# Blocked attention and two MLPs on one core: the first attention pass ordered per engine by a planner in the kernel, block sums of v on VectorE

## The chip, the cores and the metric

The kernel runs on one core of one Trainium2 chip. The metric is device time in microseconds (us), the median of the runs. Five engines run side by side, each through a queue of its own that it never reorders: TensorE (PE; its weight loads are listed as PEld), VectorE (DVE), ScalarE (ACT), GpSimd (POOL) and SyncE (SP), which here only issues transfers. An engine that waits for another holds up everything behind the waiting instruction.

## The reference

```python
k_sum = k.reshape(B, H, nb, block, D).max(axis=3)       # block = 32
v_sum = v.reshape(B, H, nb, block, D).mean(axis=3)
scores_l = scale * q @ k.T          # kept where |pos_q - pos_k| < 16
scores_s = scale * q @ k_sum.T + np.log(block)
a = softmax(concat([masked scores_l, scores_s]))        # 1e-9 added to the sum
x = a @ concat([v, v_sum])                              # (B*S, H*D) = (1536, 512)
h = x @ w_in                        # 512 -> 2048
x = (max(h, 0) + alpha * min(h, 0)) @ w_out             # first MLP
h = x @ w2_in
out = (h * sigmoid(h)) @ w2_out                         # second MLP
```

q, k and v are (2, 8, 768, 64), all float32. Each query sees a window of its neighbours and the 24 block sums of its head.

## The kernel before

**Tiling.** The 1536 tokens are six blocks of 256 (three per batch), the eight heads four pairs. One *item* is a block and a pair: 24 items, of which the first eight are blocks 0 and 1 pair by pair, then blocks 2 to 5. An item runs through all engines: `scores` (PE, tile `sc`, eight matmuls of 64 queries by 120 keys, the 120 being 24 block maxima and 96 neighbours), scaling and mask (DVE, `t`), row maximum (DVE, `nm`), `exps` (ACT, `e`, sums into `sm`), 1e-9 added to the sums and reciprocal (DVE, `sm` and `rs`), `normalize` (POOL, `e`), `turn` (PE, `pt`; copied by ACT to `pT`), `values` (PE, `o`), and the split of the result in two float32r halves (ACT `xh`, DVE `xl`). Once per batch and pair come `prep_k` (DVE, L465, block maxima of k, copied six times at L471), `prep_v1` (POOL halves the 32 elements of a block twice at L482, DVE sums the last eight at L485, `vr`) and `prep_v2` (PE transpose `pv`, four ACT copies into `vs`).

**The MLPs.** Every float32 product is made of three float32r matmuls of halves (`three`, L281 to L283). A weight piece is loaded as 64-bit numbers and converted by three DVE instructions (L142, L146, L149), an ACT cast (`wh`) and, in the first pass, a POOL subtraction (`wl`, L156). The first of the four column chunks of the first MLP is done block by block beside attention ("dense" work below): 48 matmuls of 128x256 for the inputs of a block, activation (ACT `g` and `m`, DVE L328, ACT `gh`, POOL `gl` at L337), and 48 for its outputs. Everything later is matmuls of 128x512, four chunks for each MLP; the second MLP takes some of its products by a seven-product scheme.

**What sets the order of the first pass.** Each operation is entered in a list with a key (item number plus a constant such as `AT_TURN`); the list is walked in the order of the keys, and the framework then places each instruction on its engine by a timeline of its own. So the three conversion instructions, for example, come apart in VectorE's queue. Only block 0's inputs are accumulated pair by pair as items finish (`first_in`); blocks 1 to 5 wait until all four pairs are there.

```python
AT_KEYS, AT_SUMS, AT_MEANS, AT_SPREAD = -1.1, 1.3, 2.2, 3.2
AT_EXPS, AT_NORM, AT_TURN, AT_VALUES = 0.1, 0.3, 1.8, 3.2
for _, _, f, a in sorted(ops, key=lambda o: o[:2]):
    f(*a)
```

Of the kernel before, what the change touches and what calls it, by code (L numbers as in the profile page):

```python
# [25 lines left out]
AT_KEYS, AT_SUMS, AT_MEANS, AT_SPREAD = -1.1, 1.3, 2.2, 3.2  # L26
AT_EXPS, AT_NORM, AT_TURN, AT_VALUES = 0.1, 0.3, 1.8, 3.2
AT_IN = 5.3
AT_LATER, ITEM_STEP = 3.5, 0.8
CONV, CONV_STEP = -1.4, 0.6  # L30
CONV2, CONV2_STEP = 14.0, 1.5
BATCH, BATCH_STEP = 5.8, 2.0
NQ = 6
STAGE = 2


@with_exitstack
def tile_blocks_attention_mlps(
# [19 lines left out]
    KEYS = P + 2 * PAD  # L58
# [61 lines left out]
    def conv_next(eng):  # L120
# [33 lines left out]
        def rest():  # L154
            nc.scalar.copy(out=hi, in_=w)  # L155
            eng.tensor_tensor(out=lo, in0=w, in1=hi, op=ALU.subtract)  # L156
# [5 lines left out]
        return rest  # L162
# [115 lines left out]
    def three(ps, a, b, first, last):  # L278

        (ah, all_), (bh, bl) = a, b  # L280
        nc.tensor.matmul(ps, all_, bh, start=first, stop=False)  # L281
        nc.tensor.matmul(ps, ah, bl, start=False, stop=False)  # L282
        nc.tensor.matmul(ps, ah, bh, start=False, stop=last)  # L283
# [3 lines left out]
    def in_k(u, i, k, ps):  # L287
        l, ch, t0, n, _ = u
        c = slice(i * P, (i + 1) * P)
        hi, lo = pieces[l, ch, 0, k]  # L290
        three(
            ps, (hi[:, c], lo[:, c]), (xh[:, k, t0:t0 + n], xl[:, k, t0:t0 + n]),
            k == 0, k == KT - 1,
        )
# [9 lines left out]
    def activate(u, i, ni, banks):  # L304

# [14 lines left out]
        if l == 0:  # L320
            m = gp.tile([P, 512], F32, tag="m", name="m", bufs=1 if early else 2)
            w = ni * n // len(banks)
# [3 lines left out]
            for j in range(ni):  # L326
# [5 lines left out]
        else:  # L332
            nc.scalar.activation(out=g, in_=banks[0], func=AF.Silu)

        def rest():
            nc.scalar.copy(out=gh, in_=g)  # L336
            (nc.gpsimd if early else nc.vector).tensor_tensor(out=gl, in0=g, in1=gh, op=ALU.subtract)  # L337

        pending.append(rest)
# [80 lines left out]
    def convert(eng):  # L420
        r = conv_next(eng)
        if r is not None:
            pending.append(r)
            load_next()

    NG = NBLK * NPAIR
    with ExitStack() as scope0:
# [7 lines left out]
        mask = cst[:, P:]  # L435

        kt_t, vt_t, vs_t, q_t = {}, {}, {}, {}

        def load_k(b, p):

            t = kv.tile([P, NTWO + 1, NB + KEYS], F32, tag="kT", name="kT")
            nc.sync.dma_start(out=t[:, :NTWO, NB:], in_=kT[b, p])
            kt_t[b, p] = t

        def load_v(b, p):
# [5 lines left out]
            vt_t[b, p] = t  # L451
            t = kv.tile([NC, NSUB, P], F32, tag="vs", name="vs")
            vs_t[b, p] = t
            nc.sync.dma_start(out=t[NB:, 0::2], in_=vw[b, p, 0])
            nc.sync.dma_start(out=t[:WIN, 1::2], in_=vw[b, p, 1])
# [7 lines left out]
        def prep_k(b, p):  # L463
            t = kt_t[b, p]
            nc.vector.tensor_reduce(  # L465
                out=t[:, 0, :NB].rearrange("p (n m) -> p n m", n=NTWO),
                in_=t[:, :NTWO, NB + PAD:NB + PAD + P].rearrange("p n (m i) -> p n m i", i=BLOCK),
# [7 lines left out]
        vr_t = {}  # L475

        def prep_v1(b, p):

            t = kv.tile([P, NB], F32, tag="vr", name="vr", bufs=2)
            v = vt_t.pop((b, p)).rearrange("p (n i) -> p n i", i=BLOCK)  # L480
# [7 lines left out]
        def prep_v2(b, p):  # L488
            s_ = vs_t[b, p]
# [3 lines left out]
            def spread(s0, s1):  # L493
                for at in (s_[:NB, 2 * s0:2 * s1:2], s_[WIN:, 2 * s0 + 1:2 * s1:2]):
                    nc.scalar.activation(
                        out=at,
                        in_=pt[:NB, 0:P].unsqueeze(1).to_broadcast([NB, s1 - s0, P]),
                        func=AF.Copy,
                        scale=1.0 / BLOCK,
                    )  # L500

            spread(0, QB // P)
            return lambda: spread(QB // P, NTWO)

        e_t, pt_t, sums, t_t = {}, {}, {}, {}

        def where(n):
            blk, p = order[n]
            b, j = divmod(blk, BPB)
            return blk, p, b, j  # L510

        def scores(n):
            blk, p, b, j = where(n)
            q_, k_ = q_t.pop((blk, p)), kt_t[b, p].rearrange("p n c -> p (n c)")

            ps = ps_s.tile([P, 2, 512], F32, tag="s", name="sc")
            for i in range(2):
                for h in range(2):
                    hp = slice(h * D, (h + 1) * D)
                    for s in range(2):  # L520

                        w0 = (2 * j + i) * (NB + KEYS) + s * (NB + SUB)
                        nc.tensor.matmul(
                            ps[s * SUB:(s + 1) * SUB, h, i * NC:(i + 1) * NC],
                            q_[hp, i * P + s * SUB:i * P + (s + 1) * SUB],
                            k_[hp, w0:w0 + NC],
                            start=True,
                            stop=True,
                        )
            t = att.tile([P, 4, NC], F32, tag="t", name="t", bufs=3)  # L530
            nc.vector.scalar_tensor_tensor(  # L531
                out=t.rearrange("p (h i) c -> p h (i c)", h=2),
                in0=ps[:, :, :2 * NC],
# [5 lines left out]
            nm = att.tile([P, 4], F32, tag="nm", name="nm")  # L539
            nc.vector.tensor_reduce(out=nm, in_=t, axis=AX.X, op=ALU.max, negate=True)  # L540
            t_t[n] = t, nm

        def exps(n):
            t, nm = t_t.pop(n)
            e = att.tile([P, 4, NC], F32, tag="e", name="e", bufs=3)
            sm = att.tile([P, 4], F32, tag="sm", name="sm")
            for u in range(4):
                nc.scalar.activation(  # L548
                    out=e[:, u, :], in_=t[:, u, :], func=AF.Exp, bias=nm[:, u:u + 1],
                    accum_out=sm[:, u:u + 1],  # L550
                )
            e_t[n] = e
            sums[n] = sm

        def normalize(n):
            sm, e = sums.pop(n), e_t[n]
            nc.vector.tensor_scalar(out=sm, in0=sm, scalar1=1e-9, scalar2=None, op0=ALU.add)  # L557
            rs = att.tile([P, 4, 1], F32, tag="rs", name="rs")
            nc.vector.reciprocal(out=rs.rearrange("p u o -> p (u o)"), in_=sm)
            nc.gpsimd.tensor_tensor(out=e, in0=e, in1=rs.to_broadcast([P, 4, NC]), op=ALU.mult)  # L560

        def turn(n):
            e = e_t.pop(n)
            ps = ps_mm.tile([P, 512], F32, tag="mm", name="pt")
            for u in range(4):
                nc.tensor.transpose(ps[:NC, u * P:(u + 1) * P], e[:, u, :], ident)
            t = att.tile([NC, 512], F32, tag="pT", name="pT")
            nc.scalar.copy(out=t, in_=ps[:NC])
            pt_t[n] = t

        def values(n):
            blk, p, b, j = where(n)
            t, s_ = pt_t.pop(n), vs_t[b, p]
            ps = ps_mm.tile([P, 512], F32, tag="mm", name="o")[:, :QB]
            for i in range(2):
                for s in range(2):
                    for h in range(2):
# [7 lines left out]
                        )  # L585
            at = slice(blk * QB, (blk + 1) * QB)
            nc.scalar.copy(out=xh[:, p, at], in_=ps)  # L587
            nc.vector.tensor_tensor(out=xl[:, p, at], in0=ps, in1=xh[:, p, at], op=ALU.subtract)


# [283 lines left out]
```

## Time and profile before

| what | value |
|---|---|
| median of three runs | 608.24 us (608.11 to 608.34) |
| span of the profiled execution | 604.6 us, first to last instruction |
| around the span (median less span) | 3.6 us |
| busy share of the span: PE, DVE, ACT, POOL | 95%, 70%, 46%, 12% |
| chain that ended last, by engine | PE 82%, DVE 9%, DMA 3%, ACT 2% |

The profile gives one execution by its span alone, so its own time is taken as the span and the 3.6 us around it. Busy is not the same as full speed: a matmul's length in the trace holds its way through the array, so successive matmuls overlap, and what one costs is the distance from its start to the next one's start.

### The profile page before, as it was taken

What the parts mean: (1) busy time and instruction counts of PE and PEld (TensorE: products, weight loads), DVE (VectorE), ACT (ScalarE), POOL (GpSimd) and SP (SyncE); (2) the same over time, 40 slices, a digit from 0 to 9 for tenths busy, and PEclk for the clock granted to TensorE, in tenths of its full rate; (3) what the DMA queues carried; (4) which work ended last, traced back from release to release, by engine and by line L of the source; (5) the groups of instructions that cost most, each with busy time, mean ns of one, the idle gap of its engine ahead of it and who ended that gap; (6) DMA issues with size and microseconds to landing.
All of it is one profiled execution on the core that took longest, in us unless ns stands there. A gap on an engine that the chain in (4) does not pass through costs nothing.

```text
span 604.6 us, 8927 instructions
## 1 busy us (share of the span) xinstructions
PE 576.8 (95%) x3428; PEld 483.5 (80%) x3428; DVE 424.0 (70%) x747; ACT 277.5 (46%) x636; POOL 72.3 (12%) x69
## 2 busy tenths in 40 slices
PE   2777999999999999999999999999999999999997
PEld 1556788999888888888888888888888888888886
DVE  3899979548995484349696879885972499965312
ACT  2768977654543341424544645543621245333200
POOL 2657654232100000000000000000000000000000
PEclk9988999999999999999999999999999999999999
DMA  9958754002351040003022002333130032200112
GB/s 263 341 193 260 231 147 140 2 2 70 140 154 56 0 140 0 1 1 112 28 69 70 1 1 79 131 117 93 32 108 0 1 111 96 73 1 0 54 69 88
DMA packets 31771, 52.54 MB, mean 87 GB/s; under 512 B 2288, under 2 KB 20976, under 8 KB 31728
## 3 DMA queue, kind: packets, MB, share of 16 engines
q1 hardware_dynamic: 31728, 51.97, 27.2%
q8 instruction: 27, 0.44, 0.3%
q14 instruction: 16, 0.13, 0.1%
HBM read 48.82 MB, written 3.15 MB: 86 GB/s over the span
## 4 chain that ended last, share of the span: by engine, by line
PE 82%; DVE 9%; DMA 3%; ACT 2%; SPq 1%; issue 1%; POOL 0%; DVEq 0%; POOLq 0%
PE ps L281 27%; PE ps L282 27%; PE ps L283 27%; DVE w L146 2%; DMA y<-in_w 1%; DVE w L149 1%; DMA vs<-in_vw 1%; DVE w L142 1%; DVE t L531 1%; DVE sm L557 1%; DVE nm L540 1%; PE o L579 1%; DVE kT L465 1%; ACT e L548 1%; DMA raw<-in_w 1%
## 5 line engine op out<-in xcount | busy, mean ns | idle before, releaser
L281 PE MATMUL ps<-xh,wl 128*128 128x512 f32 (+1 forms) x352 | 127.5, 367 | 1.2 <-ACT xh L587 1.2
L282 PE MATMUL ps<-xl,wh 128*128 128x512 f32 (+1 forms) x352 | 127.9, 364 | 0.0
L283 PE MATMUL ps<-xh,wh 128*128 128x512 f32 (+1 forms) x352 | 127.4, 363 | 0.0
L282 PE MATMUL ps<-gl,wh 128*128 128x512 f32 (+1 forms) x240 | 83.3, 348 | 0.0
L283 PE MATMUL ps<-gh,wh 128*128 128x512 f32 (+1 forms) x240 | 82.9, 346 | 0.0
L281 PE MATMUL ps<-gh,wl 128*128 128x512 f32 (+1 forms) x240 | 82.5, 350 | 0.0
L336 ACT CAST gh<-g 128x512 fp32r<-128x512 f32 x96 | 59.3, 622 | 46.2 <-PE ps L283 24.2
L281 PEld LDWEIGHTS ps<-xh,wl 128*128 128x128 f32 x352 | 66.5, 191 | 12.4 <-POOL e L560 1.4
L282 PEld LDWEIGHTS ps<-xl,wh 128*128 128x128 f32 x352 | 67.3, 191 | 10.2 <-issue 0.2
L283 PE MATMUL ps<-wh,gh 128*128 128x512 f32 (+1 forms) x196 | 75.4, 385 | 0.0
L283 PEld LDWEIGHTS ps<-xh,wh 128*128 128x128 f32 x352 | 67.3, 191 | 10.1
L282 PE MATMUL ps<-wl,gh 128*128 128x512 f32 (+1 forms) x196 | 75.4, 385 | 0.0
L281 PE MATMUL ps<-wh,gl 128*128 128x512 f32 (+1 forms) x196 | 75.2, 385 | 0.1
L337 DVE TENSOR_TENSOR gl<-g,gh 128x512 fp32r<-128x512 f32 x84 | 57.5, 687 | 20.7 <-ACT gh L336 20.3
L394 DVE TENSOR_TENSOR y<-ps,y 128x512 f32<-128x512 f32 x48 | 32.8, 689 | 45.4 <-PE ps L283 45.2
L324 ACT ACTIVATE g<-ps 128x512 f32<-128x512 f32 (+1 forms) x50 | 29.0, 579 | 70.8 <-PE ps L283 69.9
L155 ACT CAST wh<-w 128x512 fp32r<-128x512 f32 x64 | 39.3, 622 | 48.0 <-DVE w L149 43.5
L328 DVE SCALAR_TENSOR_TENSOR g<-m,nal,g 128x512 f32<-128x512 f32 (+1 forms) x60 | 41.4, 705 | 25.0 <-ACT m L325 24.9
L281 PEld LDWEIGHTS ps<-gh,wl 128*128 128x128 f32 x240 | 45.2, 189 | 6.6 <-issue 0.5
L282 PEld LDWEIGHTS ps<-gl,wh 128*128 128x128 f32 x240 | 45.4, 189 | 6.1 <-POOL gl L337 0.2
L283 PEld LDWEIGHTS ps<-gh,wh 128*128 128x128 f32 x240 | 45.3, 189 | 5.6
L146 DVE SCALAR_TENSOR_TENSOR w<-raw,w 128x512 uint32<-128x512 uint32 x61 | 44.6, 741 | 0.3
(82 smaller groups left out, 867.1 us busy)
## 6 DMA issues: line engine op xcount, KB each, us to landing
raw<-in_w SPq DMA_DIRECT2D x61, 512.0 KB, 3.8
vs<-in_vw SPq DMA_DIRECT2D x16, 288.0 KB, 5.6
kT<-in_kT SPq DMA_DIRECT2D x8, 480.0 KB, 5.2
q<-in_qT SPq DMA_DIRECT2D x24, 128.0 KB, 4.1
out<-y SPq DMA_DIRECT2D x11, 256.0 KB, 2.0
y<-in_vT SPq DMA_DIRECT2D x4, 384.0 KB, 6.5
y<-in_w SPq DMA_DIRECT2D x3, 512.0 KB, 7.7
raw<-in_vT SPq DMA_DIRECT2D x4, 384.0 KB, 4.5
```

Of the source, the lines that this page charges most:

```text
L142: nc.vector.tensor_scalar(out=w, in0=high, scalar1=3, scalar2=0x3FFFFFFF, op0=ALU.logical_shift_left, op1=ALU.bitwise_and,)
L146: nc.vector.scalar_tensor_tensor(out=w, in0=high, scalar=0xC0000000, in1=w, op0=ALU.bitwise_and, op1=ALU.bitwise_or)
L149: nc.vector.scalar_tensor_tensor(out=w, in0=low, scalar=29, in1=w, op0=ALU.logical_shift_right, op1=ALU.bitwise_or)
L155: nc.scalar.copy(out=hi, in_=w)
L281: nc.tensor.matmul(ps, all_, bh, start=first, stop=False)
L282: nc.tensor.matmul(ps, ah, bl, start=False, stop=False)
L283: nc.tensor.matmul(ps, ah, bh, start=False, stop=last)
L324: nc.scalar.activation(out=g[:, j * w:(j + 1) * w], in_=ps, func=AF.Relu)
L328: nc.vector.scalar_tensor_tensor(out=g[:, at], in0=m[:, at], scalar=nal[:, f + j:f + j + 1], in1=g[:, at], op0=ALU.mult, op1=ALU.add,)
L336: nc.scalar.copy(out=gh, in_=g)
L337: (nc.gpsimd if early else nc.vector).tensor_tensor(out=gl, in0=g, in1=gh, op=ALU.subtract)
L394: nc.vector.tensor_tensor(out=at, in0=src, in1=at, op=ALU.add)
```

## The change

The first pass is cut into steps, each of one engine, with a cost, the steps that it needs, the buffers that it takes and gives, and a key. `plan()` in the kernel orders them engine by engine, before anything is issued: at each turn it takes the step that can start first, the smaller key where several can within 0.03. Steps marked `lock` (the three conversion instructions, the DVE half of the activation, and every POOL step) are never planned beside each other. The instructions are then issued in that order with the framework's reordering off (`manual_schedule`). After the pass, the framework orders as before.

Moved and changed beside the order:

- The block sums of v are one DVE reduction over 768 elements (`sum_v`, 32 at a time); POOL's 16 halving instructions go.
- k is loaded once without the overlap (800 columns, 0.41 MB, in place of 960), the maxima stand behind it, and L471's eight copies go. The scores of an item are now 4 matmuls of 128 queries by 24 maxima and 8 of 64 queries by 96 neighbours. The neighbours' v is one transfer in place of two.
- The 1e-9 lies in a second column beside the sum, and a DVE reduction over two elements adds them, where a scalar add stood.
- v's means are spread by two ACT copies in place of four.
- Blocks 0 and 1 both accumulate their inputs pair by pair. Two inputs of the next chunk (`next_in`) are issued at the end of the pass.

```diff
-AT_KEYS, AT_SUMS, AT_MEANS, AT_SPREAD = -1.1, 1.3, 2.2, 3.2
+AT_KEYS, AT_SUMS, AT_MEANS, AT_SPREAD = -1.5, 2.21, 2.18, 3.06
-    KEYS = P + 2 * PAD
+    KEYS = S + 2 * PAD
...
-            nc.vector.tensor_copy(
-                out=t[:, 1:, :NB], in_=t[:, 0:1, :NB].to_broadcast([P, NTWO, NB])
-            )
...
-            for w in (BLOCK // 2, BLOCK // 4):
-                nc.gpsimd.tensor_tensor(
-                    out=v[:, :, :w], in0=v[:, :, :w], in1=v[:, :, w:2 * w], op=ALU.add
-                )
+        def sum_v(b, p, w):
+            t = kv.tile([P, NB], F32, tag="vr", name="vr", bufs=2)
+            v = vt_t.pop((b, p)).rearrange("p (n i) -> p n i", i=BLOCK)
             nc.vector.tensor_reduce(out=t, in_=v[:, :, :w], axis=AX.X, op=ALU.add)
...
+                for h in range(2):
+                    hp = slice(h * D, (h + 1) * D)
+                    nc.tensor.matmul(
+                        ps[:, h, i * NC:i * NC + NB],
+                        q_[hp, i * P:(i + 1) * P],
+                        k_[hp, KEYS:KEYS + NB],
+                        start=True,
+                        stop=True,
+                    )
...
-            nc.vector.tensor_scalar(out=sm, in0=sm, scalar1=1e-9, scalar2=None, op0=ALU.add)
+            nc.vector.tensor_reduce(out=r, in_=sm, axis=AX.X, op=ALU.add)
+            nc.vector.reciprocal(out=r, in_=r)
...
+                step(("vr", b, p), "DVE", 0.87, [("vt", b, p)], k + AT_SUMS, sum_v, b, p, BLOCK,
+                     take=["vr"], give=["raw"] * (b > 0))
...
+            step(("cv", n), "DVE", 1.65, [("W", n)] + [("cv", n - 1)] * (n > 0), t, bits, n,
+                 take=["w"], give=["raw"] * (n >= y_w.shape[1]), lock=True)
...
+                        at = max([free[e], *(end[x] for x in after)])
+                        for r in take:
+                            at = max(at, sorted(hold[r])[take.count(r) - 1])
+                        if lock:
+                            at = max(at, locked)
...
-        for _, _, f, a in sorted(ops, key=lambda o: o[:2]):
-            f(*a)
+        with tc.manual_schedule():
+            for _, _, f, a in plan():
+                f(*a)
```

Two places show what moves. First VectorE's queue, behind the block maxima of the fourth pair; `w` is a weight being converted, `sm`, `rs` and `eps` the softmax sums and their reciprocals, `xl` the low half of an item's result. Before:

```order
L557 TENSOR_SCALAR sm<-sm 128x4
L485 TENSOR_REDUCE vr<-y 128x24
L540 TENSOR_REDUCE nm<-t 128x4
L559 RECIPROCAL rs<-sm 128x4
L142 TENSOR_SCALAR w<-raw 128x512
L146 SCALAR_TENSOR_TENSOR w<-raw,w 128x512
L149 SCALAR_TENSOR_TENSOR w<-raw,w 128x512
L142 TENSOR_SCALAR w<-raw 128x512
L557 TENSOR_SCALAR sm<-sm 128x4
L588 TENSOR_TENSOR xl<-o,xh 128x256
L146 SCALAR_TENSOR_TENSOR w<-raw,w 128x512
```

The same place in the changed kernel:

```order
L488 TENSOR_REDUCE kT<-kT 128x24
L556 SCALAR_TENSOR_TENSOR t<-sc,cst 128x480
L507 TENSOR_REDUCE vr<-y 128x24
L583 TENSOR_REDUCE rs<-eps_94 128x4
L584 RECIPROCAL rs<-rs 128x4
L567 TENSOR_REDUCE nm<-t 128x4
L627 TENSOR_TENSOR xl<-o,xh 128x256
L556 SCALAR_TENSOR_TENSOR t<-sc,cst 128x480
L146 TENSOR_SCALAR w<-y 128x512
L150 SCALAR_TENSOR_TENSOR w<-y,w 128x512
L153 SCALAR_TENSOR_TENSOR w<-y,w 128x512
```

Before, the fourth and fifth weights stand here; now it is the second, its three instructions together, and an item's steps come first. When VectorE reaches the eighth `xl`, it has finished eight conversions and most of a ninth before, four now. Second, TensorE's queue in the middle of the first eight items (`pt` a transpose, `o` the values, `ps` dense work). Before:

```order
L282 MATMUL ps<-xl,wh 128x256
L283 MATMUL ps<-xh,wh 128x256
L566 MATMUL pt<-cst,e 120x128 x4
L523 MATMUL sc<-kT,q 64x120 x8
L579 MATMUL o<-pT,vs 64x64 x8
```

and now:

```order
L612 MATMUL o<-pT,vs 64x64 x8
L287 MATMUL ps<-xh,wl 128x256
L288 MATMUL ps<-xl,wh 128x256
L289 MATMUL ps<-xh,wh 128x256
L287 MATMUL ps<-xh,wl 128x256
L288 MATMUL ps<-xl,wh 128x256
```

Dense work now follows every one of the first eight items (12 matmuls each, 96 in all), where before only block 0's 48 stood between them, sometimes split by an item's matmuls.

## Rows read from the trace of the kernel before

**Rows 1.** The profile page: its first line and busy time by engine.

```profile
span 604.6 us, 8927 instructions
PE 576.8 (95%) x3428; PEld 483.5 (80%) x3428; DVE 424.0 (70%) x747; ACT 277.5 (46%) x636; POOL 72.3 (12%) x69
```

**Rows 2.** Windows, last stretch: length, busy us of each engine, clock, DMA share, GB/s.

```profile
150.00:601.00 451.00, 450.90 (x2022) 374.51 (x2021) 307.68 (x516) 177.51 (x309) 1.53 (x1) 1.00 0.18 61
```

**Rows 3.** Timeline of TensorE, late in the pass and at the end: start, us.

```profile
117.63 0.64 PE L523 MATMUL sc<-kT,q 64*64 64x120 f32 x16
118.20 0.69 PE L579 MATMUL o<-pT,vs 120*64 120x64 f32 x16
118.82 0.65 PE L566 MATMUL pt<-cst,e 128*120 128x128 f32 x4
119.40 0.69 PE L579 MATMUL o<-pT,vs 120*64 120x64 f32 x16
...
590.05 0.39 PE L282 MATMUL ps<-wl,gh 128*128 128x512 f32 x1
...
594.13 0.39 PE L282 MATMUL ps<-wl,gh 128*128 128x512 f32 x1
...
601.03 0.28 PE L282 MATMUL ps<-wl,gh 128*128 128x256 f32 x1
601.15 0.28 PE L283 MATMUL ps<-wh,gh 128*128 128x256 f32 x1
```

**Rows 4.** Windows, VectorE alone: length, busy us and count, clock, DMA.

```profile
0.00:73.40 73.40, 61.69 (x125) 0.95 0.86 259
```

**Rows 5.** Groups by line, VectorE, first 73.4 us: busy us, mean ns, idle before.

```profile
L465 DVE TENSOR_REDUCE kT<-kT 128x24 f32<-128x768 f32 x8 | 7.5, 943 | 6.4 <-DMA kT<-in_kT 6.4
...
L557 DVE TENSOR_SCALAR sm<-sm 128x4 f32<-128x4 f32 x15 | 6.4, 425 | 0.0
```

**Rows 6.** Timeline of VectorE, 57 to 65 us: start, us.

```profile
57.25 0.93 DVE L465 TENSOR_REDUCE kT<-kT 128x24 f32<-128x768 f32 x1
58.11 0.41 DVE L588 TENSOR_TENSOR xl<-o,xh 128x256 fp32r<-128x256 f32 x1
...
58.53 0.61 DVE L540 TENSOR_REDUCE nm<-t 128x4 f32<-128x480 f32 x1
59.07 0.76 DVE L557 TENSOR_SCALAR sm<-sm 128x4 f32<-128x4 f32 x1
...
59.89 0.64 DVE L531 SCALAR_TENSOR_TENSOR t<-sc,cst 128x480 f32<-128x480 f32 x1
60.46 0.41 DVE L142 TENSOR_SCALAR w<-raw 128x512 uint32<-128x512 uint32 x1
...
61.42 1.24 DVE L146 SCALAR_TENSOR_TENSOR w<-raw,w 128x512 uint32<-128x512 uint32 x1
...
63.77 0.34 DVE L485 TENSOR_REDUCE vr<-raw 128x24 f32<-128x192 f32 x1
64.03 0.15 DVE L557 TENSOR_SCALAR sm<-sm 128x4 f32<-128x4 f32 x1
64.10 0.68 DVE L149 SCALAR_TENSOR_TENSOR w<-raw,w 128x512 uint32<-128x512 uint32 x1
64.70 0.47 DVE L328 SCALAR_TENSOR_TENSOR g<-m,nal,g 128x256 f32<-128x256 f32 x1
```

**Rows 7.** Timeline of GpSimd, same stretch: start, us.

```profile
58.82 0.98 POOL L560 TENSOR_TENSOR e<-e,rs 128x480 f32<-128x480 f32 x1
...
61.12 0.99 POOL L560 TENSOR_TENSOR e<-e,rs 128x480 f32<-128x480 f32 x1 [0.70 <-DVE rs L559]
```

**Rows 8.** Timeline of TensorE, early: start, us, and its idle time before.

```profile
5.66 1.34 PE L523 MATMUL sc<-kT,q 64*64 64x120 f32 x16 [5.66 <-DVE kT L465]
...
54.90 1.08 PE L523 MATMUL sc<-kT,q 64*64 64x120 f32 x16
```

**Rows 9.** DMA issues: KB each, median us from issue to landing.

```profile
raw<-in_vT SPq DMA_DIRECT2D x4, 384.0 KB, 4.5
```

More of the change, by code (lines that the diff above doesn't have):

```diff
@@ L304, in activate, with activation @@
     def activate(u, i, ni, banks):
+        one, two, *rest = activation(u, i, ni, banks)
+        one()
+        two()
+        pending.extend(rest)
+    def activation(u, i, ni, banks):
         l, ch, t0, n, _ = u
@@ L331, in activate, with three_, four @@
                 )
-        else:
-            nc.scalar.activation(out=g, in_=banks[0], func=AF.Silu)
-        def rest():
+        def three_():
             nc.scalar.copy(out=gh, in_=g)
+        def four():
             (nc.gpsimd if early else nc.vector).tensor_tensor(out=gl, in0=g, in1=gh, op=ALU.subtract)
-        pending.append(rest)
+        return one, two, three_, four
     turn_g = [0]
@@ L730, in seq_item, with step, load @@
-        def seq_item():
-            need(CF if seq[0][1] is in_item else 2 * CF)
-            item()
-        def more_loads():
-            for _ in range(CF):
-                ask(None)
+        where = {g: k for k, g in enumerate(order)}
+        steps = []
+        def step(name, engine, cost, after, key, f, *a, take=(), give=(), lock=False, size=0):
+            steps.append((key, len(steps), name, engine, cost, after, f, a, take, give, lock, size))
+        def load(name, key, f, *a, size, after=(), take=()):
+            step(name, "SP", 0.6, after, key, f, *a, take=take, size=size)
@@ new lines, in tile_blocks_attention_mlps @@
+        room = {"sc": 1, "mm": 6, "t": 3, "e": 3, "pT": 2, "q": NQ, "k": 4, "v": 4, "vr": 2,
+                "raw": STAGE, "w": 2, "g": 1, "gh": 3}
+        at = 0
+        n = 0
+        for p in range(NPAIR):
+            load(("k", 0, p), -100 + at, load_k, 0, p, size=0.41, take=["k"])
+            load(("q", 0, p), -100 + at + 0.1, load_q, 0, p, size=0.13, take=["q"])
+            if p == 0:
+                load("cst", -100 + at + 0.2, lambda: nc.sync.dma_start(out=cst, in_=consts), size=0.31)
+            load(("vt", 0, p), -100 + at + 0.3, load_vt, 0, p, size=0.39)
+            load(("v", 0, p), -100 + at + 0.4, load_v, 0, p, size=0.6, take=["v"])
+            load(("q", 1, p), -100 + at + 0.5, load_q, 1, p, size=0.13, take=["q"])
+            at += 1
@@ new lines, in tile_blocks_attention_mlps @@
+        for n in range(3 * CF + STAGE):
+            t = W_FIRST + n * W_STEP if n < 2 * CF else max(W_FIRST + n * W_STEP, CONV2 + (n - 2 * CF) * CONV2_STEP - W_AHEAD)
+            load(("W", n), t, load_next, size=0.52, after=[("W", n - 1)] * (n > 0),
+                 take=["raw"] * (n >= y_w.shape[1]))
+        load("al", -80, lambda: nc.sync.dma_start(out=al, in_=alpha), size=0.01)
+        step("nal", "POOL", 0.1, ["al"], 0, lambda: nc.gpsimd.tensor_scalar(out=nal, in0=al, scalar1=-1.0, scalar2=None, op0=ALU.mult))
@@ L846, in _layout @@
         "qT": turned(q),
[L847 removed]
+        "kT": kp,
         "vT": turned(v),
```

445 lines of the change are left out of this document (250 added, 195 removed).

## Prediction

> **What bounds the kernel now.** Read the profile's first page, then the windows, then the timelines. TensorE is busy 95% of the span [rows 1], and from 150 us to 601 us without a gap (450.90 of 451.00) [rows 2]. So the time is TensorE's work plus what TensorE loses, and the losses lie at the start. To size them I price each matmul by the distance from its start to the next start, late in the run, where nothing is waited for [rows 3]: a 128x512 matmul 0.2267 us (18 of them between 590.05 and 594.13), a 128x256 one 0.12, an item's scores 0.57, its values 0.62, its transposes 0.58. The program holds 1956 of the first (443.4), 600 of the second (72.0), 24 items (24 x 1.77 = 42.5) and eight small transposes (a quarter of 0.58 each, 1.2): 559.0 us. The last matmul starts at 601.15, so TensorE is done at 601.3 and has lost 42.3 us. 3.3 us of tail follow to the end of the span, and 3.6 us more make the median of 608.24, against which the sum is made.
>
> Where is the loss made? VectorE runs the first pass. Its row lengths overlap the next row by some 0.08 us, so again start to start [rows 6]: block maxima 0.86, `xl` 0.33, `nm` 0.54, `t` 0.57, a sum of v over 192 elements 0.26, an `sm` or another small row 0.07, a conversion 0.33 + 0.60 + 0.60 = 1.53, half an activation 0.40. Up to the end of the second activation of block 0, at 73.4 us, its queue holds 8 maxima (6.9), 16 `t` (9.1), 16 `nm` (8.6), 6 sums of v (1.6), 9 conversions (13.8), 11 `xl` (3.6), 4 activation halves (1.6) and 36 small rows (2.5): 47.7 us. TensorE's queue holds 15 scores, 12 transposes, 10 values, 4 small transposes and 72 dense matmuls up to the matmuls that need this activation: 30.9 us. By order alone VectorE is 47.7 - 30.9 = 16.8 us behind there. It was busy 61.69 of the 73.4 us [rows 4], so it idled 11.7, 6.4 of it until a load of k landed [rows 5], and 61.7 - 47.7 = 14.0 went into rows that were longer than their price. 16.8 + 11.7 + 14.0 = 42.5: the whole loss of the run.
>
> **The change, term by term.**
>
> *Order.* In the new queues the farthest that VectorE lies behind TensorE is at the scores of the nineteenth item, which need the eighteenth `t`. Up to it VectorE has 8 maxima (6.9), 18 `t` (10.3), 17 `nm` (9.2), 8 sums of v, 7 conversions (10.7), 12 `xl` (4.0), 6 activation halves (2.4) and 34 small rows (2.4). A sum over 768 elements does not occur before; I price it as the maximum over the same 768 [rows 6], 0.86, so 6.9 where the short sums cost 2.1: 4.8 us more work in all, bounded below by 0.26 and above by the row's whole length, 0.93. Total 52.8. TensorE has 18 scores at 0.75 (below), 14 transposes, 14 values, 7 small transposes and 120 dense matmuls: 45.7. Lag 7.1 in place of 16.8. That is the largest term: conversions come later and dense work of block 1 earlier.
>
> *Idle.* Loads of k are 0.41 MB in place of 0.48, and no sum waits for GpSimd any more; but VectorE still has nothing before the first k. 11.7 becomes 9.5, between 7 and 11.7.
>
> *Lengthened rows.* An `sm` of 0.15 took 0.76 us beside GpSimd's `e`, which ran from 58.82 to 59.80, and a conversion's second instruction 1.24 beside the `e` at 61.12, where its sister took 0.68 [rows 6, 7]. The fifteen `sm` average 425 ns, 4.1 us too long together, while the maxima average 943 beside a free 930 [rows 5, 6]: a reduction is not lengthened. The new sum of two is a reduction, so 4.1 of the 14.0 go for good. Of the other 9.9, seven conversions in place of nine would leave 7.7; GpSimd's halving, part of the cause, is gone, and the plan keeps the rest apart, but on paper only, since no semaphore does. I take 5. Against it, rows that need each other's result now stand back to back (some 37 pairs); at the 0.07 by which neighbours otherwise overlap that is 2.5, an estimate. 14.0 becomes 7.5, between 2.5 and 12.4.
>
> The Trainium skill's SBUF page ("Who interferes with whom") says that VectorE and GpSimd take one port pair by an exclusive lock, that the loser stands still, and that a `tensor_reduce` never takes part. The rows above agree. By that rule alone, were the plan's gaps kept, this term would be 2.5 and the time 589; were they not, 10.2 and 597.
>
> *Scores.* An item's sixteen records (two for a matmul) take 0.57, so 0.036 each; the new form has 24. If a record's price is fixed, an item costs 0.86; if only columns count it costs no more than before. I take 0.75, nearer the first since the narrow ones carry twice the queries: +0.18 x 24 = 4.3 us of TensorE work, between 0 and 6.8.
>
> The skill's page TensorEngine Tiling (Array Packing), "Instruction Overhead", speaks against this part: a matmul has some 60 cycles of overhead, so 24 columns cost what 60 do. By it, as an estimate, eight records of 25 ns add 0.2 us an item, 4.8 us in all, and the time would be 595. No run here has shown a 24-column matmul yet.
>
> *Free.* GpSimd's sixteen halvings and two of four spreading copies of ScalarE leave engines that are busy 12% and 46% [rows 1]; they count only through the two terms above. The eight copies of the maxima are among the small rows. One transfer of neighbours in place of two takes eight issues off SP, which I put at nothing: SP waits for buffers, not for its own issue. After the pass nothing changes, and TensorE is full there as before [rows 2].
>
> *Sum.* Loss 7.1 + 9.5 + 7.5 = 24.1 in place of 42.3. 559.0 + 4.3 + 24.1 = 587.4, plus 3.3 and 3.6: **594.3 us**, 14 less than 608.24.
>
> **Rivals.**
>
> *A new wait in the fixed order.* VectorE's sum of v for the last pair of batch 1 waits for a load that SP issues behind the neighbours' v of that pair, and that needs the buffer which the twelfth item's values free. TensorE reaches those values after some 37 us of work, at 61 with its loss; two issues and 4.5 us of landing [rows 9] give 67 to 68. VectorE is there after 51 us of work and 17 lost, at 68. There is no room: if TensorE is late, VectorE stands with all `t` behind it. Price up to one landing, 4.5: 599. For it: nothing can now be moved around a late transfer. Against it: the sums were late before as well, without stopping the pass.
>
> *The plan's gaps are not kept.* `lock` exists only in the plan. Then lengthening stays at 14.0 - 4.1 + 2.5 = 12.4, 4.9 more: 599. For it: GpSimd runs `e` at any moment when sums are ready [rows 7]. Against it: seven conversions stand where nine did.
>
> *More than forecast.* Gaps kept and the narrow scores hidden: 594.3 - 5.0 - 4.3 = 585.
>
> *Slower: TensorE stays at its lower clock.* The first scores take 1.34 us, and those at 54.90 still 1.08 [rows 8], against 0.64 for the same row later [rows 3]: 1.2 GHz after the engine had waited, 2.4 GHz when it had worked on. The granted clock of the first 73.4 us is 0.95 in the windows [rows 4], which does not show all of this. Today the low clock is covered by VectorE's lag. With only 7 us of lag it would not be: were all 45.7 us run at half speed from the start at 5.7, TensorE would be at the nineteenth scores at 97.1, having lost 51.4 in place of 24.1: 621.6. It decides from the point where 5.7 plus the work at half speed passes the loss that gives today's time (24.1 + 13.9 = 38.0), so from 32 of the 45.7 us. Against it: twelve dense matmuls now follow every early item, which is what kept the clock up late in the pass.
>
> **How the numbers follow.** Forecast (589 to 599) 0.60; more than forecast (583 to 589) 0.14; new wait 0.10; gaps not kept 0.07 (both 599 to 603, where the forecast's terms are also a little worse); low clock 0.06; several small losses that add up to no change 0.03. Less than 0.2% (1.2 us) cannot be told from no change. Faster: 0.60 + 0.14 + 0.10 + 0.07, less 0.01 for a wait at its worst, 0.90; same 0.03; slower 0.07. The bounds of the terms reach from 594.3 - 2.5 - 5.0 - 4.3 = 582.5 to 594.3 + 2.2 + 4.9 + 2.5 = 603.9; 585 to 603 leaves out the low clock, no change and the best part of the best case, together under 0.2.
>
> **What would show it.** VectorE: sums over two at 0.15 and none near 0.7; sums over 768 at 0.93; conversions of about 1.6 from start to end; idle under 10 us by 70. TensorE: its last values near 120 us with dense work of two blocks behind it, no wait over 2 us after 50, scores of 0.7 to 0.8 in full stretches. Wrong would be: scores above 0.9, groups of 1.1 beyond 40 us (low clock), VectorE waiting for `raw` around 60 to 70, or conversions still at 2 us or more.

## The result: slower, 616.3 us where 594.3 was predicted

| | median of the runs | ratio to before, 95% interval |
|---|---|---|
| before | 608.17 us (607.67 to 608.34) | |
| the change | 616.31 us (613.69 to 619.24) | 1.0135 [1.0091, 1.0179] |
| the change, measured again | 614.72 us (608.33 to 618.32) | 1.0066 [1.0029, 1.0102] |

The second set had its own executions of before (median 609.57 us), and its ratio leaves out one execution of the change that stood in a slower state of the chip (618.32). So the change is slower by 0.7 to 1.4%, and it lies 12 to 13 us outside the prediction's range (585 to 603). The profiled execution took 618.46 us, 1.76 more than its span. Every execution on record has some 1.8 us around its span, so before's profiled one (span 604.6) would have taken about 606.4, which is 1.8 us less than the median and half of the 3.6 us that the prediction put around the span.

The profile page of the change, against [rows 1]:

```profile
span 616.7 us, 9237 instructions
PE 598.2 (97%) x3620; PEld 502.8 (82%) x3620; DVE 417.4 (68%) x743; ACT 275.1 (45%) x616; POOL 55.6 (9%) x53
```

TensorE is busy 21.4 us longer and VectorE 6.6 us shorter. Windows of the change (length, busy us of PE, PEld, DVE, ACT and POOL with their instructions, granted clock, DMA share, GB/s), against [rows 2, 4]:

```profile
0.00:73.40 73.40, 61.64 (x702) 49.80 (x702) 47.73 (x104) 43.79 (x149) 19.75 (x24) 1.00 0.76 218
...
150.00:612.00 462.00, 460.76 (x2147) 384.01 (x2146) 318.67 (x536) 185.02 (x324) 4.07 (x3) 1.00 0.18 61
```

In the first 73.4 us VectorE is busy 47.73 us where it had been busy 61.69, so it idles 25.7 us there, 11.7 before. (The granted clock, the 1.00 near the end of the first line, does not show that TensorE's rows up to 45 us ran at half speed; the rows below do.) Nor are VectorE's rows long. Its groups in the first 73.4 us (busy us, mean ns, idle before), against [rows 5, 6]:

```profile
L556 DVE SCALAR_TENSOR_TENSOR t<-sc,cst 128x480 f32<-128x480 f32 x14 | 9.2, 655 | 19.6 <-PE sc L544 19.6
...
L150 DVE SCALAR_TENSOR_TENSOR w<-raw,w 128x512 uint32<-128x512 uint32 x3 | 2.1, 693 | 0.1
...
L583 DVE TENSOR_REDUCE rs<-eps 128x4 f32<-128x8 f32 x13 | 2.0, 153 | 0.0
L507 DVE TENSOR_REDUCE vr<-raw 128x24 f32<-128x768 f32 x2 | 1.9, 944 | 0.0
```

The sum over two takes 153 ns where the `sm` took 425, a conversion's second instruction 693 where one had taken 1240 (1100 on average over the six from `raw`), the new sum of v 944. Instead `t` waited 19.6 us for TensorE's scores. They are what grew. TensorE's timeline (start, length in us), one item at the lower clock, one at the upper, and the end, against [rows 3, 8]:

```profile
18.53 0.63 PE L533 MATMUL sc<-kT,q 64*128 64x24 f32 x4
19.08 0.60 PE L544 MATMUL sc<-kT,q 64*64 64x96 f32 x8
19.61 0.62 PE L533 MATMUL sc<-kT,q 64*128 64x24 f32 x4
20.16 0.60 PE L544 MATMUL sc<-kT,q 64*64 64x96 f32 x8
20.69 1.12 PE L612 MATMUL o<-pT,vs 120*64 120x64 f32 x16
...
51.28 0.41 PE L533 MATMUL sc<-kT,q 64*128 64x24 f32 x4
51.62 0.40 PE L544 MATMUL sc<-kT,q 64*64 64x96 f32 x8
51.94 0.41 PE L533 MATMUL sc<-kT,q 64*128 64x24 f32 x4
52.27 0.40 PE L544 MATMUL sc<-kT,q 64*64 64x96 f32 x8
52.60 0.65 PE L596 MATMUL pt<-cst,e 128*120 128x128 f32 x4
...
613.34 0.28 PE L289 MATMUL ps<-wh,gh 128*128 128x256 f32 x1
```

An item's scores take 52.60 - 51.28 = 1.32 us, before 0.57; at the lower clock 2.16, before 1.08. "64\*128" is the part of the array that a matmul uses, rows by columns; inside an item TensorE now goes over from one to the other three times. Values (0.62) and transposes (0.58) cost what they did. 24 x 0.75 = 18.0 us of work were added.

For each kernel below I made the same account of TensorE up to 152 us: its work over before's 559.0 us; its waits (the brackets in its timeline); and what rows at half speed took over their price at the upper clock, start to start. The fillers of e10 are matmuls on zeros, counted with the time that they took. All in us, of the profiled execution, which is one out of each kernel's scatter (e6's is among its slower ones, e17's its fastest), so these spans do not rank the kernels as the medians do:

| kernel | scores of an item | added work | waits | half speed | sum | span |
|---|---|---|---|---|---|---|
| before | 0.57 | 0 | 25.7 | 14.9 | 40.6 | 604.6 |
| the change | 1.32 | 18.0 | 14.0 | 18.6 | 50.6 | 616.7 |
| e1, old scores | 0.57 | 0 | 25.6 | 15.2 | 40.8 | 605.5 |
| e6, 64x24 scores | 0.73 | 3.8 | 22.3 | 14.5 | 40.6 | 605.4 |
| e2, grouped | 1.05 | 11.5 | 15.1 | 15.2 | 41.8 | 607.6 |
| e4, 64x120 | 1.40 | 19.9 | 14.5 | 8.7 | 43.1 | 609.0 |
| e10, e6 and fillers | 0.73 | 3.8 + 11.2 | 13.9 | 7.9 | 36.8 | 602.2 |
| e17, e6 with less VectorE work | 0.73 | 3.8 | 19.3 | 9.3 | 32.4 | 595.7 |

The span less the sum is 563.3 to 566.1 us in all eight, where before's work and tail are 562.3: 1 to 4 us are in none of the columns, and the kernels agree to 3 us. TensorE's waits fell from 25.7 to 14.0, and the longer scores added 18.0. The waits did not fall by the new order alone: with before's scores and layouts in it (e1) they are 25.6.

### The profile page after: what moved, and what is told of

It is laid out like the page before. It is cut to its first block, busy times and chain, and to the rows that moved or that the text cites. A ratio compares the mean times of both kernels' runs of the same rounds, so it can differ in the third digit from the quotient of the medians.

```text
span 616.7 us, 9237 instructions
## 1 busy us (share of the span) xinstructions
PE 598.2 (97%) x3620; PEld 502.8 (82%) x3620; DVE 417.4 (68%) x743; ACT 275.1 (45%) x616; POOL 55.6 (9%) x53
## 4 chain that ended last, share of the span: by engine, by line
PE 90%; DVE 3%; DMA 2%; ACT 2%; issue 1%; POOL 0%; SPq 0%; POOLq 0%; ACTq 0%; DVEq 0%
PE ps L287 27%; PE ps L288 27%; PE ps L289 27%; PE sc L533 3%; PE sc L544 3%; PE o L612 2%; PE pt L596 2%; DMA q<-in_qT 1%; DVE g L347 1%; DMA raw<-in_w 1%; DVE w L150 1%; ACT g L341 1%; DVE t L556 0%; POOL gl L356 0%; ACT m L342 0%
## 5 line engine op out<-in xcount | busy, mean ns | idle before, releaser
L287 PE MATMUL ps<-xh,wl 128*128 128x512 f32 (+1 forms) x352 | 131.4, 373 | 0.0
L288 PE MATMUL ps<-xl,wh 128*128 128x512 f32 (+1 forms) x352 | 129.6, 368 | 0.0
L289 PE MATMUL ps<-xh,wh 128*128 128x512 f32 (+1 forms) x352 | 129.5, 368 | 0.0
L287 PEld LDWEIGHTS ps<-xh,wl 128*128 128x128 f32 x352 | 69.2, 197 | 10.8
L288 PEld LDWEIGHTS ps<-xl,wh 128*128 128x128 f32 x352 | 69.3, 197 | 10.1 <-DVE xl L627 0.2
L289 PEld LDWEIGHTS ps<-xh,wh 128*128 128x128 f32 x352 | 69.1, 196 | 10.0
L341 ACT ACTIVATE g<-ps 128x512 f32<-128x512 f32 x48 | 28.7, 598 | 72.5 <-PE ps L289 68.8
L347 DVE SCALAR_TENSOR_TENSOR g<-m,nal,g 128x512 f32<-128x512 f32 (+1 forms) x60 | 38.8, 663 | 28.5 <-ACT m L342 28.3
L159 ACT CAST wh<-w 128x512 fp32r<-128x512 f32 x64 | 39.3, 621 | 41.6 <-DVE w L153 37.1
L574 ACT ACTIVATE e<-t,nm 128x120 f32<-128x120 f32 x96 | 36.6, 383 | 15.8 <-DVE nm L567 15.1
```

The lines of the kernel that those rows point to most:

```text
L287: i = nc.tensor.matmul(ps, all_, bh, start=first, stop=False, skip_group_check=again)
L288: nc.tensor.matmul(ps, ah, bl, start=False, stop=False, skip_group_check=again)
L289: nc.tensor.matmul(ps, ah, bh, start=False, stop=last, skip_group_check=again)
L341: nc.scalar.activation(out=g[:, j * w:(j + 1) * w], in_=ps, func=AF.Relu)
L347: nc.vector.scalar_tensor_tensor(out=g[:, at], in0=m[:, at], scalar=nal[:, f + j:f + j + 1], in1=g[:, at], op0=ALU.mult, op1=ALU.add,)
L574: nc.scalar.activation(out=e[:, u, :], in_=t[:, u, :], func=AF.Exp, bias=nm[:, u:u + 1], accum_out=sm[:, u, 0:1],)
```

## Experiments

The edits are shown in short, not word for word. Each run was timed beside before, whose median was 609.1 to 609.7 us in these sets; the ratios are to that.

### What the scores cost: e1, e2, e4, e5, e6

**e1** puts before's scores and layouts into the new order.

```diff
-    4 matmuls q[64 x 128], maxima[64 x 24];  8 matmuls q[64 x 64], window[64 x 96]
+    8 matmuls q[64 x 64], [24 maxima | 96 neighbours][64 x 120]
```

> The change with the scores of before: eight 64x120 matmuls an item instead of four 128x24 and eight 64x96, and with them the layouts of before (stacked k with its copies of the block maxima, vw in two transfers, spread in two activations an half); the planned order, VectorE's sums of v and the eps tiles stay. Theory W, a small fp32 matmul costs by the columns of its stationary tile (64 queries .07 us, 128 queries .15 to .17): an item's scores fall from 1.31 back to 0.57 us at the upper clock and from 2.16 to 1.08 at the lower, 24 x 0.74 = 17.8 us leave TensorE's work, and the time is 597 to 602 us, faster than both kernels. Rival O, the new order or the clock costs the time and the scores only show it (operands that arrive piecemeal inside an item): an item stays over 1.0 us and the time stays at 612 or above.

605.91 us (ratio to before 0.994 [0.9912, 0.9968]); an item 0.57 again. So the scores' form, with the layouts that belong to it, is the difference between slower and faster (rival O falls), but only 9 to 10 of the 18 us come through, less than theory W's 597 to 602 asked for: TensorE's waits are back at 25.6.

**e2** issues the 128x24 matmuls of both halves first.

```diff
     for i in range(2):
         for h in range(2): matmul 128x24
+    for i in range(2):
         for h in range(2):
             for s in range(2): matmul 64x96
```

> The change with the four 128x24 matmuls of an item issued first and the eight 64x96 behind them, so that TensorE goes over between the two tile shapes once inside an item instead of three times. Theory W (stationary columns): nothing changes, an item's scores 1.31 us, time within 3 us of the change (613 to 619). Rival S, each going-over between tile shapes costs: of the 0.74 us more than before, 0.28 is four records' worth each way and the rest, about 0.46, lies in four goings-over of 0.115, so two fewer give 1.08 us an item and 24 x 0.23 = 5.5 us less, 611.

606.53 us (0.9957 [0.9931, 0.9983]). TensorE's timeline of e2:

```profile
54.00 0.63 PE L533 MATMUL sc<-kT,q 64*128 64x24 f32 x8
54.56 0.56 PE L545 MATMUL sc<-kT,q 64*64 64x96 f32 x16
55.05 0.69 PE L613 MATMUL o<-pT,vs 120*64 120x64 f32 x16
```

The same matmuls take 0.56 + 0.49 = 1.05 us where they took 1.32. Only their order changed, and with it the number of goings-over, from three inside an item to one: 0.135 us each. Theory W (the columns of the stationary tile) falls, and S stands in the price (it gave 1.08). In time 8 to 10 us follow, more than the 6.5 us of work: in the profiled executions rows at half speed took 3.4 us less as well.

**e4** widens the windows; the extra columns are written over or read by nobody.

```diff
-    ps[.., i * NC + NB:(i + 1) * NC],      k_[hp, w0:w0 + WIN]
+    ps[.., i * NC + NB:(i + 1) * NC + NB], k_[hp, w0:w0 + NC]
```

> The change with every 64x96 score matmul widened to 64x120 moving columns (the 24 more land where the next 128x24 writes over them or in columns that nobody reads). Theory W (stationary columns): an item's scores stay at 1.31 us (the 64x96 records at 41 ns, as before's 64x120 had 36), time within 3 us of the change. Rival M, moving columns set the price: the sixteen records' 0.65 us grow by a quarter, 0.16 us an item, 24 x 0.16 = 3.9 us more, about 620.

612.16 us (1.006 [1.0032, 1.0088]), an item 1.40. A quarter more moving columns costs 0.08 us an item, half of rival M's price and more than W's nothing: columns count, but little. The time did not rise with it (0.6% above before, the change 0.7 to 1.4%): in e4's profiled execution rows at half speed took 8.7 us, in the change's 18.6. So the clock can be worth several us between two executions.

**e5** adds the four 128x24 matmuls to before; the 64x120 ones write over them.

```diff
     for i in range(2):
+        for h in range(2): matmul 128x24
         for h in range(2):
             for s in range(2): matmul 64x120
```

> The kernel before with four 128x24 matmuls more in every item's scores, which the 64x120 matmuls then write over: the added work alone, in the old order. Theory W: an item's scores go from 0.57 to 1.25 to 1.35 us at the upper clock and from 1.08 to about 2.2 at the lower, and since most of before's items lie between work of TensorE's own, the time grows by 10 to 20 us, 618 to 628. Rival R, a price per record (.036 us): eight records more an item, 0.86 us an item, 24 x 0.29 = 6.9 us, at most 615. Rival O (only the new order makes them dear): an item stays under 0.75, at most 612.

642.33 us (1.054 [1.0519, 1.0561]), an item 1.40 as in e4. In the old order, where TensorE stands between others' work, 24 x 0.83 = 20 us of work cost 33 us, beyond all three forecasts. Its items still ran at the lower clock at 71.7 us, before's last at 54.90 [rows 8].

**e6** makes each 128x24 matmul as two of 64x24, so that all sixteen have the tile shape 64\*64.

```diff
-    ps[:, h, i * NC:i * NC + NB],  q_[hp, i * P:(i + 1) * P]
+    ps[s * SUB:(s + 1) * SUB, h, i * NC:i * NC + NB],  q_[hp, i * P + s * SUB:i * P + (s + 1) * SUB]
```

> The change with each 128x24 score matmul made as two of 64x24, so that all sixteen matmuls of an item have the tile shape 64x64 and TensorE never goes over between shapes inside the scores; the stationary columns that are loaded stay the same. Theory S (a going-over between tile shapes costs about 0.135 us, two fewer gave 1.32 to 1.05): the eight 64x96 cost 0.49 us, the eight 64x24 from half of a 128x24's 0.106 us (0.053, if the stationary columns set the price) to 0.061 us (a 64x96's), so an item takes 0.91 to 0.98 us, and with 24 x 0.1 = 2.4 us less than the grouped version (606.5) the time is 602 to 607. Rival R (a price per matmul of the 24 columns, 0.106 us, whatever its shape): 0.85 + 0.49 = 1.34 us an item, time as the change or above, 612 to 619.

605.35 us (0.9917 [0.9883, 0.9951]). TensorE's timeline of e6:

```profile
53.53 0.31 PE L534 MATMUL sc<-kT,q 64*64 64x24 f32 x8
53.67 0.37 PE L545 MATMUL sc<-kT,q 64*64 64x96 f32 x8
53.87 0.26 PE L534 MATMUL sc<-kT,q 64*64 64x24 f32 x8
53.95 0.38 PE L545 MATMUL sc<-kT,q 64*64 64x96 f32 x8
54.26 0.69 PE L613 MATMUL o<-pT,vs 120*64 120x64 f32 x16
```

0.73 us: below what S gave. Twice the matmuls with 24 columns take 0.14 + 0.08 = 0.22 us, where e2's four took 0.56. Of those 0.34 one going-over is 0.135; the other 0.2 are left for the 64\*128 form itself.

### What else the change did: e7, e8, e9

**e7** is e1 with the sums of v halved by GpSimd again, as before.

```diff
+    step(("hv", b, p), "POOL", 1.65, [("vt", b, p)], k + AT_SUMS - 0.5, halve_v, b, p, lock=True)
-    step(("vr", b, p), "DVE", 0.87, [("vt", b, p)], k + AT_SUMS, sum_v, b, p, BLOCK,
+    step(("vr", b, p), "DVE", 0.26, [("hv", b, p)], k + AT_SUMS, sum_v, b, p, BLOCK // 4,
```

> The version with the old scores, and GpSimd halves v twice as before, so that VectorE's last sum is over 8 and takes 0.26 us instead of 0.87; all else as there (605.9 us). Theory V, with the short scores VectorE is the next bound of the first 90 us: 8 x 0.61 = 4.9 us less on it give 2 to 5 us, 601 to 604. Rival D, the loads are (8 to 12 us of TensorE's idle time lie behind kT and q): 605 to 607. Rival L, GpSimd's eight halvings of 1.67 us lengthen VectorE's rows as in the kernel before: 607 to 610.

611.76 us (1.0026 [1.0, 1.0052]), 6 us slower than e1, so beyond rival L. TensorE's waits rise from 25.6 to 30.1. VectorE has less work, but by 80 us its rows are some 12 us over their prices, in e1 some 9. That is half of the 6 us; the plan's order differs too, and the rest is not traced. The change's sums of v by VectorE alone are worth some 6 us here.

**e8** gives e1's planner the durations of the trace, **e9** does that to e7.

```diff
-    "K" 0.87, "sc" 0.8,  "pt" 0.45, "o" 0.88, load of k 0.41
+    "K" 1.25, "sc" 0.57, "pt" 0.58, "o" 0.62, load of k 0.49
```

> The version with the old scores, its planner given the durations that the trace shows (scores 0.57 instead of 0.8, values 0.62 instead of 0.88, transposes 0.58 instead of 0.45, K with its copies 1.25 instead of 0.87, a load of k 0.49 instead of 0.41). Theory P, the plan's wrong costs leave steps queued in a bad order: 2 us or more less than 605.9, 600 to 604. Rival, the bound is the work of the other engines and the loads, and no order removes it: 604 to 608.

> Both edits, the halvings on GpSimd and the measured costs, on the version with the old scores. If theories V and P hold, their gains add: 597 to 602. If only V: as the version with the halvings alone. If the loads bound it: 604 to 607.

611.95 (1.0035 [1.0015, 1.0055]) and 616.12 us (1.0109 [1.0087, 1.0132]): 6 us worse than e1, 4 worse than e7. True durations with the other constants left alone make a worse plan; the keys were evidently set together with the costs they stand beside. That is argued, not shown. Theory P falls for this version. The plan holds an item's scores at 0.8 us, near e6's 0.73; whether the change would gain by a plan with its true 1.32 was not tried.

### Where the rest of the gain stayed: e10 to e18

e6 has scores at 0.73 us, the forecast had 0.75: it is the forecast kernel, and yet 605, not 594. Three suspects were taken away one by one.

**The early low clock: e10 (on e6), e11 (on the change), e13 (on before); e12 is the change once more.**

```diff
+    for n, times in enumerate((14, 14, 4, 6)):
+        step(("wu", n), "PE", 0.0, [("sc", *order[n - 1])] * (n > 0), -200, warm_up, times)   # 128x128 on zeros
```

> The version with 64x24 scores (605.35 us), and 38 matmuls of 128x128 on zeros, whose results nobody reads, put where TensorE waits at the start: 14 before the first scores, 14 behind them, 4 and 6 behind the second and third items'. Theory C, TensorE's lower clock in the first 40 us is on the path (14.5 us went to rows at half speed in that version): with work in the gaps the clock rises earlier, rows after 15 us stand at the upper clock, and 4 to 9 us go: 596 to 601. Rival B, what the low clock takes is covered, since loads and VectorE set the pace of the first 40 us: rows may be faster, TensorE waits instead, 603 to 607. Slower by more than 2 us, if the added matmuls delay the first scores.

> The change itself with the same 38 matmuls on zeros. Theory C: the stretch at the lower clock, which reached to 45 us in the profiled run, ends before 20 us; of the 18.6 us that rows at half speed took 6 to 10 go, since here TensorE hardly waits for anybody between 17 and 60 us: 606 to 610. Rival B: no more than 2 us, 613 or above.

> The change, unaltered, once more on the chip of this comparison: 613 to 619 us, and the length of its stretch at the lower clock against its time. Theory C: where the stretch ends near 30 us in place of 45, the time is 5 us or more below the 618.5 of the run profiled first. Rival: the time stands at 618 wherever the stretch ends.

> The kernel before with the same matmuls on zeros (here the scheduler places them, most before the second item). In the old order TensorE waits for GpSimd and VectorE again and again up to 54 us, so by theory B nothing is gained (607 to 610); by theory C up to the 8.7 us that rows at half speed took before 34 us, less what VectorE's lag takes back: 602 to 606.

603.98 us (0.9915 [0.9891, 0.994]), 616.99 (1.0133 [1.0097, 1.0169]), 614.72 (above) and 619.40 (1.0159 [1.013, 1.0187]). TensorE's timeline of e10:

```profile
7.33 3.39 PE L465 MATMUL wu<-warm 128*128 128x128 f32 x28
...
10.96 0.31 PE L542 MATMUL sc<-kT,q 64*64 64x24 f32 x8
11.06 0.41 PE L553 MATMUL sc<-kT,q 64*64 64x96 f32 x8
...
22.95 0.43 PE L542 MATMUL sc<-kT,q 64*64 64x24 f32 x8 [1.76 <-DVE kT L496]
```

In e6:

```profile
11.60 0.43 PE L534 MATMUL sc<-kT,q 64*64 64x24 f32 x8 [1.21 <-DMA q<-in_qT]
11.81 0.60 PE L545 MATMUL sc<-kT,q 64*64 64x96 f32 x8
```

The scores at 10.96 run at the upper clock, where those of e6 at 11.60 ran at the lower, and half-speed rows fall from 14.5 to 7.9 us, in the change from 18.6 to 8.0. But at most 1.4 us of time come of it in e10, within the scatter, and none in e11. TensorE arrives earlier and waits (the 1.76), and the fillers have a price of their own: waits and fillers together are 25.1 us in e10, where e6's waits are 22.3, and the first scores start at 6.6 us, in e6 at 4.8. Rival B stands for this way of raising the clock; what a higher clock without the fillers' price would bring, no run shows. In before (e13) the fillers delay, and rows run at half speed up to 56 us all the same, so it tells nothing of an earlier clock. In e12 the profiled execution again had its lower clock to 45 us, so it tells nothing of another length.

**The wait for weights: e14 (on e6), e15 (on the change), e16 (on e10).** In e6 a turned v of batch 1 holds one staging buffer, so a weight is asked for only when the conversion before it has freed the other. SyncE's issues (start, us) and VectorE's next conversion in e6:

```profile
64.19 0.33 SPq L120 DMA_DIRECT2D raw<-in_w  x1
```

```profile
73.54 0.43 DVE L146 TENSOR_SCALAR w<-raw 128x512 uint32<-128x512 uint32 x1 [3.61 <-DMA raw<-in_w]
```

```diff
-    t = stage.tile(.., name="raw") ..      # turned v of batch 1
+    t = kv.tile([P, S], F32, tag="vtb", name="vtb", bufs=2)
```

> The version with 64x24 scores (605.35 us), and the turned v of batch 1 is loaded into two buffers of its own, not into the two that the weights are staged in. In the trace of that version one of the staging buffers holds a turned v from 30 to 77 us, so each weight is asked for only when the conversion before it has freed the other (at 50.23 and 64.19 us), lands 4.1 and 9.3 us later behind four loads of neighbours, and VectorE stands at 70 to 73.5 with the t of later items behind it. Theory Q (this wait is what keeps the order's gain from coming): the conversions find their weights there, VectorE's waits for raw between 40 and 90 us go, and the time is 597 to 602 us. Rival: VectorE's work, or the low clock, takes it up again: 603 to 607.

> The same edit on the change itself (614.7 to 616.3 us). Theory Q as a part of the loss after 60 us: its waits for raw (1.2 at 61 and 1.9 at 79.6 us) and TensorE's 1.6 at 73 go, with the low clock behind them (some 3.7 us between 75 and 94): 608 to 613. Rival W, TensorE's own work with its scores of 1.32 us sets the pace alone: 613 to 619.

> Own buffers and the 38 matmuls on zeros together, on the 64x24 version. If the early clock's gain (6 us of rows at half speed, of which 1.4 came through) was taken by the wait for weights, the two add: 593 to 599, near what was predicted for the change. If not, as with own buffers alone, less 1 to 2 us.

605.58 (0.9958 [0.9932, 0.9984]), 616.15 (1.013 [1.008, 1.0181]) and 608.69 us (0.998 [0.9956, 1.0005]). Theory Q falls in all three; with the fillers, the buffers even cost some 4 us (e16 against e10). The plan orders anew when buffers are free, so the wait's own worth is not seen by itself. It takes conversions earlier: by 60 us VectorE has done some 43 us of work at its prices, in e6 39, and TensorE waits for `t` instead. Waits of TensorE, 15 to 110 us (us in total, times, longest), in e6 and in e14:

```profile
PE sc L534 <- DVE t L557: 3.5, 3, 2.0
```

```profile
PE sc L534 <- DVE t L557: 7.7, 3, 6.3
```

**VectorE's own work: e17 (on e6), e18 (on the change).** The maxima and the sums of v read a quarter of their elements; the order stays.

```diff
-    in_=t[:, PAD:PAD + S] .. (p, n, i)          in_=v[:, :, :w]
+    in_=t[:, PAD:PAD + S] .. [:, :, :BLOCK // 4]    in_=v[:, :, :w // 4]
```

> The version with 64x24 scores (605.35 us), in which the eight block maxima of k and the eight sums of v read a quarter of their elements (192 in place of 768; three quarters of both are left out of what is computed). Nothing else moves: 16 x 0.61 = 9.8 us less work on VectorE alone, at the same place in the same queues. Theory V (with the short scores VectorE is what bounds the pass, whatever is removed elsewhere): TensorE's waits for t and kT shrink and half or more of it comes through, 596 to 601. Rival D (the loads at the start and behind 60 us, and the low clock, bound it): 603 to 607.

> The same on the change itself (614.7 to 616.3 us). Theory V for the change: VectorE idles 25 of its first 70 us, most of it behind TensorE's scores, so 9.8 us less work there bring at most 3: 612 to 617. Rival: VectorE bounds the change too, and 5 us or more go: 606 to 611.

600.30 us (0.9844 [0.9813, 0.9875]) and 611.48 (1.0033 [1.0005, 1.006]). Of 9.8 us taken from VectorE alone 5 come through in e6 and 3 to 5 in the change. Theory V holds for e6, by half; for the change the time lies between V's 612 to 617 and the rival's 606 to 611. VectorE's work is the only one of the three that clearly moved the time. In the account the gain is not VectorE's alone: from e6 to e17 waits fall by 3.0 us and rows at half speed by 5.2.

## Why the prediction was wrong

**The step that failed first is *Scores*.** It priced a matmul by its records, 0.57 to 0.86 us an item, and took 0.75. Measured: 1.32, outside both bounds, 24 x (1.32 - 0.75) = 13.7 us more TensorE work than in the sum. What was missing is that the two kinds of matmul use the array in two shapes. Before's rows show one shape inside the scores and so no price for going over [rows 3]; the bounds were made from records of that one shape and held to be bounds of another. e2 and e6 show both parts: three goings-over at 0.135 us, and the 64\*128 form. With them removed the forecast price is met (0.73), the change is no longer slower than before, and 9 to 11 of the 20 to 22 us between forecast and measurement are gone.

The Trainium skill's page TensorEngine Tiling (Array Packing) had it, not in the section that the prediction quoted but in "Key Properties": a change of the tiling mode, not merely of the tile, drains TensorE. e2 agrees with it, at 0.135 us a change. The quoted rule, that 24 columns cost what 60 do, gave by the prediction's estimate 0.2 us for the eight records of four 128x24 matmuls; in e2 they took 0.56 with one going-over. e6's eight 64x24 matmuls are sixteen records and took 0.22: near the estimate's 0.2 when matmuls are counted, half of its 0.4 when records are. The 0.77 that it gave an item is near e6's 0.73, with matmuls of one shape.

**The second is *Idle*, and the *Sum* built on it.** In e6 TensorE lost 605.4 - 562.8 - 3.3 = 39.3 us, where 24.1 were forecast and before had lost 42.3. Take the prediction's view at 80 us in e6, just behind its nineteenth scores (79.1). VectorE's window there, and its wait for a weight shown above:

```profile
0.00:80.00 80.00, 58.83 (x128) 0.92 0.86 237
```

TensorE's waits are 22.0 and its half-speed rows 10.7, so 32.7 are lost by then. VectorE's rows are 5.2 over price (58.8 busy, 53.6 at its prices; forecast *Lengthened rows* 7.5), VectorE is idle 21.2 (*Idle* 9.5), and 6.3 are left for lag (*Order* 7.1). Two of three terms came out near, the lag only as a remainder. VectorE's idle did not: 9.8 of it lies before 15 us, most of it behind the first loads, as before, and 11.4 after it, most of it behind TensorE's scores (4.4) and weights (3.9). Another 6.6 us went after 80 us, 3.8 of them rows at half speed and 2.5 in no column of the account; the prediction held 24.1 for the loss of the whole run. Its fault was to treat VectorE as the one engine in front: it subtracted what VectorE gained and let TensorE's clock and the loads be covered by the lag that the change removes. Against before (16.8 and 14.0), *Order* and *Lengthened rows* did give up 19.3 us by then; 9.5 of them came back as idle (21.2 where before had 11.7), 6.6 went after 80 us, and some 3 remained. Taken away singly, clock and weights gave at most 1.4 us (e10, e14), VectorE's work half of itself (e17). No single wait holds the missing 11 us, and how they divide is not settled.

**The table above shows the same from TensorE's side.** In the new order, scores of 0.57 (with before's layouts), 0.73 and 1.05 us give 605.9, 605.4 and 606.5: up to there TensorE's work is nearly free, because its waits shrink by about as much (25.6, 22.3, 15.1). From 1.05 to 1.32 they shrink by 1.1 only, rows at half speed grow by 3.4, and 6.5 us of work cost 8 to 10.

Point by point: *Free* was right as far as it can be seen: no wait for SyncE's issue shows, and TensorE is full after 150 us but for 1.2 us (460.76 of 462). *Lengthened rows* was about right; e7 shows a part of it from the other side. The **new wait** was there but small, 0.5 us for the turned v; a wait for weights behind the same buffers stood where it was looked for. Waits of VectorE in the change:

```profile
DVE w L146 <- DMA raw<-in_w: 3.1, 2, 1.9
...
DVE vr L507 <- DMA raw<-in_vT: 0.5, 1, 0.5
```

**Gaps not kept** did not happen. The **low clock** rival was right in what it saw, items of 2.16 us up to 45 us, one of the marks of "wrong" in the prediction. As the main cause it does not stand: rows at half speed took 3.7 us more than in before (18.6 against 14.9), and with them down to 8.0 in e11 the time stood at 617, though with the fillers' 11 us in it. The chance of 0.07 for slower was too small, since it rested on that one mechanism; "scores above 0.9", the mark that came true, had no rival of its own.

## What to carry to other kernels

When a matmul is split, look at which part of the array each piece uses: pieces of different shapes in turn cost more than their columns and records, and doing them in one shape, even with twice as many matmuls, took 0.22 in place of 0.56 us. A bound from rows of one form is no bound for another. And where two engines are nearly level, what an edit takes from one can come back as its idle time: sum the gains only up to the second engine's work, and price the start's loads and clock as terms of their own.

e6 beats both kernels: 605.35 us, 0.8% below before, 1.5 to 1.8% below the change; with fillers (e10) 603.98.

## What the runs showed of the hardware

- Going over between the array shapes 64\*128 and 64\*64 took 0.135 us at the upper clock; four 128x24 matmuls in a row 0.56 us, eight of 64x24 0.22.
- Fillers on zeros brought the upper clock before 11 us, where it had come after 27 (e6) or 45 us (the change); it fell again later, in e10 at 23 us after a wait of 1.76. In the change, after waits of TensorE of 1.6 and 0.8 us, rows went back to half speed at 75.8 and 86.5 us, and the granted clock from 75 to 95 us was 0.74 (behind the engines' busy times; then DMA share and GB/s):

```profile
75.00:95.00 20.00, 19.22 (x202) 17.00 (x196) 15.99 (x34) 15.83 (x54) 9.59 (x9) 0.74 0.62 181
```

- Some kernels in the planned order scatter more: e6's nine runs went from 599.65 to 607.99 us, e12's, without the one set aside above, from 608.33 to 617.13, before's 23 and 15 beside them from 607.1 to 613.1 and 607.75 to 611.56. Others do not (e8 611.25 to 614.0, e9 615.88 to 616.56). No run here explains it.
